# Linear attention and a two-layer FFN on one core: VectorE's first stage in written order, the key sums of nine pairs on TensorE, the second stage's first x chunk fetched and cast in the first stage

## The chip, the cores and the metric

One core of a Trainium2 chip runs the whole kernel. The metric is device time in microseconds of one execution, the median of several runs. Five engines share the core's on-chip memory: TensorE (PE, with its weight loads PEld), VectorE (DVE), ScalarE (ACT), GpSimd (POOL) and SyncE (SP), which here only issues DMAs. Each engine works its own instructions off in the order in which the program put them there, and waits for others by semaphores.

## The reference

```python
def phi(x):
    proj = einsum('bhsd,df->bhsf', x, w_phi)
    proj = proj - max(abs(proj), axis=-1)
    return concatenate([exp(proj), exp(-proj)], axis=-1)

q_p, k_p = phi(q), phi(k)
kv  = einsum('bhsf,bhsd->bhfd', k_p, v)
z   = sum(k_p, axis=2)
num = einsum('bhsf,bhfd->bhsd', q_p, kv)
den = einsum('bhsf,bhf->bhs', q_p, z)[..., None] + 1e-6
x   = (num / den), heads joined: 4608 tokens x 512
h   = x @ w_in                      # 512 -> 2048
g   = maximum(h, 0) + alpha * minimum(h, 0)
out = g @ w_out                     # 2048 -> 512
```

There are 8 batches of 8 heads, 576 tokens a head, head width 64, 128 features (256 with both signs). All data is float32.

## The kernel before, in words

The kernel has two stages, and works on transposed data (features on the 128 partitions, tokens along the free side).

**Attention.** Two heads of a batch make a pair: 32 pairs, four to a batch. `attention_units` (L192) returns a pair's work as small units, each with a due time in units of one pair (the table `AT`, L57). For pair i these stand at i plus:

- `load` (-0.95): keys and queries (`raw`, 576 KB) and values (`v`) from memory.
- `project` (five chunks, at 0 to 0.60, L202): TensorE multiplies token tiles by `w_phi` into one of two PSUM buffers `pj`; VectorE takes the largest magnitude of each row (`m`, L221) and subtracts it (`t`, L222), which frees the buffer. Chunks 0, 1 and 2 hold the k tiles (4 + 1 with 64 rows), chunks 2, 3 and 4 the queries.
- `k_exp` (0.30 and 0.48): ScalarE writes exp(t) and exp(-t) to `xk` (one buffer, L236) and to `k4` (the fifth k tile, two buffers, its lower half zero).
- `k_sum` (0.50, L241): VectorE adds the five k tiles to one, in three additions, `y` (128x1024), `z` and `z` (128x512).
- `k_acc` (0.90, L250): TensorE accumulates kv over the five tiles. `k_z` (1.150, L263): a matmul with a matrix of ones for each head turns `z` into the sums over tokens, in the same PSUM tile.
- `kv_out` (1.153), `kv_turn` (1.52), `q_exp` (1.66 to 1.80): copies and transposes; `qf` (two buffers) holds the features of the queries.
- `den` (2.149) and `num` (2.152): the denominators and numerators of the pair. ScalarE copies the denominators, and SyncE sends them through a transfer to a 128x9 layout (`d9`, L326) in the same unit.
- `invert` (2.50, L329): VectorE adds EPS and takes the reciprocal; SyncE writes it to memory (`rec_d`, L334) and reads it back broadcast over the partitions (`rr`, two transfers, L337).
- `finish` (2.85, L341): GpSimd multiplies (VectorE for the last pair), SyncE stores the pair's part of x (`x_d`, L344).

**FFN, first part.** Numbers enter matmuls as two rounded parts (`rnd` and `low`, L92 and L97), so that each product takes three matmuls (L372 to L374 up, L378 to L380 down). Of the 16 blocks of d_ff the first five (`NF1`) are taken by `ffn1_units` (L382), for chunks of 512 tokens: `fetch` loads x of the chunk (`xr`, one buffer, 1 MB, L388), `split` casts it in four parts (`xh` on VectorE, L395, `xl` on GpSimd, L397), 20 steps `up` and 20 steps `down` follow, three matmuls each; after the last `up` of a block `act_g` (L158) issues two Relus on ScalarE, a combination on VectorE (L163), a cast on ScalarE and a subtraction on VectorE. The results go to `part_d`. Chunks 0 to 6 run in the first stage, spread between the attention units: chunk c starts at `max(4c + FB, F0 + c*FR)` (9.0, 12.3, 15.6, 18.9, 22.8, 26.8, 30.8), its fetch `FL` = 0.5 and its split `FX` = 0.25 ahead.

**Weights.** They come as 64-bit numbers, in half blocks of 256 columns: `decode_load` (L122, `raww`, two buffers), and `decode` (L129): a scaling on ScalarE, four integer instructions on VectorE (L139 to L142), an addition on GpSimd, a cast on ScalarE, a subtraction on GpSimd, and for later blocks a store to `w_d`. In the first stage 20 half blocks are due every 0.5 from 0.55 on, and 20 more between 11 and 31, each load 0.5 ahead.

**The order.** All units go to one list, `todo` (L437), sorted by due time and issued in that order (L455). `tc.manual_schedule` (L456) keeps TensorE and SyncE in just this order. On the other engines the compiler's own scheduler orders the instructions, except where `keep_in_program_order` names one.

**Second stage.** `load_x(0)` (L484, L510) loads the first chunk of x in four transfers and casts it: `rnd` on ScalarE, `low` on VectorE. `pass2` (L547) then runs `up2` and `down2` over the other 11 blocks for nine chunks; after the first block of chunk 0, chunks 7 and 8 of the first part and more weight decoding follow (L560). `load_w2` (L461) brings stored weights back through GpSimd's queue.

Of the kernel before, what the change touches and what calls it, by code (L numbers as in the profile page):

```python
# [55 lines left out]
QH_BUFS = 2  # L56
AT = dict(  # L57
# [3 lines left out]
    ks=0.50,  # L61
# [7 lines left out]
    dv=2.50,  # L69
    x=2.85,  # L70
)
F0 = 9.0
FR = 3.3
FB = 6.8
FL = 0.5
FX = 0.25
# [3 lines left out]
def fused_kernel(ctx: ExitStack, tc: tile.TileContext, kq, v, w_phi, w_in, w_out, alpha, out):  # L80
# [48 lines left out]
    def decode(ff, z, o, n):  # L129
        tag = f"w{ff}_{z}_{o}"  # L130
        if (ff, z, o) not in wraw:
            decode_load(ff, z, o, n)
        raw = wraw.pop((ff, z, o))
        cs = slice(o, o + n)
        lo, hi = raw[:, :, 0], raw[:, :, 1]
        a = w1t.tile([P, n], U32, tag="wa", name=f"a{tag}", bufs=W_BUFS)
        e = w1t.tile([P, n], U32, tag="we", name=f"e{tag}", bufs=W_BUFS)
        act.activation(f(a), hi.bitcast(F32), AF.Copy, scale=2.0**-112)
        dve.tensor_scalar(a, a, 3, None, op0=ALU.logical_shift_left)  # L139
        dve.scalar_tensor_tensor(a, hi, 0x80000000, a, op0=ALU.bitwise_and, op1=ALU.bitwise_or)  # L140
        dve.tensor_scalar(e, a, 0xFF800000, None, op0=ALU.bitwise_and)
        dve.scalar_tensor_tensor(f(e), lo, 2.0**-52, f(e), op0=ALU.mult, op1=ALU.mult)  # L142
        pool.tensor_tensor(f(a), f(e), f(a), op=ALU.add)
        if ff in W:
            th, tl = W[ff][2 * z][:, cs], W[ff][2 * z + 1][:, cs]
        else:
            t = w1t.tile([P, 2, n], F32R, tag="wo", name=f"o{tag}", bufs=1)
            th, tl = t[:, 0, :], t[:, 1, :]
        rnd(act, th, f(a))
        low(pool, tl, f(a), th)  # L150
        if ff not in W:
            nc.sync.dma_start(w_d[ff - NF1, :, 2 * z : 2 * z + 2, cs], f(t))
# [5 lines left out]
    def act_g(ps, ff, n, gp, bufs, tag, el, g_bufs=G_BUFS):  # L158
        r = gp.tile([P, n], F32, tag="r", name=f"r{tag}", bufs=G_BUFS)
        g = gp.tile([P, n], F32, tag="g", name=f"g{tag}", bufs=g_bufs)  # L160
        act.activation(r, ps, AF.Relu, scale=-1.0)  # L161
        act.activation(g, ps, AF.Relu)  # L162
        dve.scalar_tensor_tensor(g, r, aln[:, ff : ff + 1], g, op0=ALU.mult, op1=ALU.add)  # L163
        gh = gp.tile([P, n], F32R, tag="gh", name=f"gh{tag}", bufs=bufs)
        gl = gp.tile([P, n], F32R, tag="gl", name=f"gl{tag}", bufs=bufs)
        rnd(act, gh, g)
        low(el, gl, g, gh)
        return gh, gl
# [23 lines left out]
    def attention_units(i):  # L192
# [48 lines left out]
        def k_sum():  # L241
            x = c["x", 0].rearrange("p a h n f -> p (a h) (n f)")
            y = wk.tile([P, 4, 2 * FD], F32, tag="y", name=f"y{i}", bufs=1)
            z = wk.tile([P, 4, FD], F32, tag="z", name=f"z{i}", bufs=1)
            dve.tensor_tensor(y, x[:, :, : 2 * FD], x[:, :, 2 * FD :], op=ALU.add)
            dve.tensor_tensor(z, y[:, :, :FD], y[:, :, FD:], op=ALU.add)
            dve.tensor_tensor(z, z, c["x", 1].rearrange("p a h n f -> p (a h) (n f)"), op=ALU.add)
            c["z"] = z.rearrange("p (a h) f -> p a h f", a=2)
# [62 lines left out]
        def den():  # L311
            ps_d = ps_m.tile([P, HS], F32, tag="m", name=f"d{i}")
            for a in range(2):
                for g in range(4):
                    h, u = divmod(g, 2)
                    pe.matmul(
                        ps_d[32 * g : 32 * g + 32, :],
                        lhsT=c["st"][:, 2 + a, h * D : h * D + 32],
                        rhs=c["qf"][:, h, a, u * HS : (u + 1) * HS],
                        start=a == 0,  # L320
                        stop=a == 1,
                    )
            d = st.tile([P, HS], F32, tag="d", name=f"ds{i}", bufs=1)
            act.copy(d, ps_d)
            d9 = st.tile([P, 9], F32, tag="d9", name=f"d9_{i}")
            nc.sync.dma_start(d9, d.rearrange("(g r) (p j) -> g r p j", r=32, j=9)[:, 0])  # L326
            c["d9"] = d9

        def invert():  # L329
            d9 = c["d9"]  # L330
            r9 = st.tile([P, 9], F32, tag="r9", name=f"r9_{i}")
            tc.keep_in_program_order(dve.tensor_scalar(d9, d9, EPS, None, op0=ALU.add))
            dve.reciprocal(r9, d9)
            nc.sync.dma_start(rec_d[i].rearrange("(p j) -> p j", j=9), r9)  # L334
            c["r"] = st.tile([P, S], F32, tag="r", name=f"rr{i}", bufs=2)
            for h in range(2):
                nc.sync.dma_start(  # L337
                    c["r"][h * D : (h + 1) * D], rec_d[i : i + 1, h * S : (h + 1) * S].broadcast_to([D, S])
                )

        def finish():  # L341
            e = dve if i == NPAIR - 1 else pool
            e.tensor_tensor(c["s"], c["s"], c["r"], op=ALU.mult)  # L343
            nc.sync.dma_start(x_d[hp, :, b * S : (b + 1) * S], c["s"])  # L344
# [9 lines left out]
            (AT["ks"], k_sum),  # L354
            (AT["kr"], kv_turn),
            (AT["n"], num),
            (AT["d"], den),
            (AT["dv"], invert),
            (AT["x"], finish),
        ]  # L360
# [21 lines left out]
    def ffn1_units(c):  # L382
# [7 lines left out]
        def split():  # L390
            xh = xhl.tile([P, NK, C2], F32R, tag="xh", name=f"xh1_{c}", bufs=1)
            xl = xhl.tile([P, NK, C2], F32R, tag="xl", name=f"xl1_{c}", bufs=1)
            for n in range(NK - 1, -1, -1):
                ins = rnd(dve, xh[:, n], xr[0][:, n])
                if c < B - 2:  # L395
                    tc.keep_in_program_order(ins)
                last[0] = low(pool, xl[:, n], xr[0][:, n], xh[:, n])  # L397
            gs.append([(xh[:, j], xl[:, j]) for j in range(NK)])

        cur = {}  # L400

        def up(ff, n):
            if n == 0:
                cur["ps"] = psf.tile([P, C2], F32, tag="f", name=f"h1_{c}_{ff}")
            ps = cur["ps"]
            gemm1(ps, W[ff], gs[0], (n,))
            if n == NK - 1:
                gs.append(act_g(ps, ff, C2, g1p, GB, f"1_{c}_{ff}", dve, 3))

        def down(m, ff):  # L410
# [6 lines left out]
            o = g1p.tile([P, C2], F32, tag="g", name=f"os1_{c}_{m}", bufs=3)  # L417
            act.copy(o, ps)
            nc.sync.dma_start(part_d[m, :, cs], o)

        steps = [lambda ff=ff, n=n: up(ff, n) for ff in range(NF1) for n in range(NK)]
        steps += [lambda m=m, ff=ff: down(m, ff) for m in range(NK) for ff in range(NF1)]
        return [fetch, split], steps

# [11 lines left out]

    todo = []  # L437
    for i in range(NPAIR):
        todo += attention_units(i)
    for b in range(B - 1):  # L440
        fl, fu = ffn1_units(b)
        t0, t1 = (max(c * NP + FB, F0 + c * FR) for c in (b, b + 1))
        todo += [(t0 + (t1 - t0) * n / len(fu), u) for n, u in enumerate(fu)]
        todo += [(t0 - FL, fl[0]), (t0 - FX, fl[1])]
    first = [(ff, z, o) for z in range(2) for ff in range(NF1) for o in range(0, 512, WN)]
    for n, blk in enumerate(first):
        t = WA + WS * n
# [33 lines left out]
    xs, prt, po = {}, {}, {}  # L481
    x2b = []

    def load_x(c):  # L484
        cs = slice(c * C2, (c + 1) * C2)
        xs[c] = []
        if c > 0:
            xr4 = x2b[0].tile([P, NK, C2], F32, tag="xr", name=f"xr{c}")
            ld_ = nc.sync.dma_start(xr4, x_d[:, :, cs].rearrange("k p s -> p k s"))
            if c > 1:  # L490
                tc.keep_in_program_order(ld_)
        for j in range(NK):
            if c > 0:
                xr = xr4[:, j]
            else:
                xr = x2p.tile([P, C2], F32, tag="xr", name=f"xr{c}{j}", bufs=NK)
                nc.sync.dma_start(xr, x_d[j, :, cs])
# [12 lines left out]
    load_x(0)  # L510
# [7 lines left out]
    def up2(c, ff):  # L518
        ps = psf.tile([P, C2], F32, tag="f", name=f"h2_{c}_{ff}")
        gemm1(ps, W[NF1 + ff], xs[c])  # L520
        gq[c, ff] = act_g(ps, NF1 + ff, C2, x2p, G2_BUFS, f"2_{c}_{ff}", dve)
# [38 lines left out]
    for c in range(B - 1, NC2):  # L560
        loads, units = ffn1_units(c)
        if c == B - 1:
            for u in loads:
                u()
# [3 lines left out]
        else:  # L568
            tail += loads + units
# [58 lines left out]
```

## Time and profile before

| what | us |
|---|---|
| median of 3 runs | 1289.01 (1287.61 to 1291.89) |
| the profiled execution | 1286.31 |
| its span, first to last instruction | 1284.5 |
| PE busy | 1201.5 |
| VectorE busy | 661.7 |
| ScalarE busy | 553.7 |
| GpSimd busy | 205.1 |

Groups, waits and stretches all come from the one profiled execution. A group's line names the line of code, the engine and the operation, then the tile written and the tiles read, shapes, count, total and mean. A line of the waits names who waited for what: total us, times, longest. In a timeline stands the start, the duration, the engine and the instruction, and in brackets the idle time of the engine before it and what ended that. A stretch gives its length, then for PE, PEld, DVE, ACT and POOL the busy time with the count of instructions, then the granted TensorE clock as a share of full speed, the DMA share and GB/s.

Matmuls overlap in the records: one is shown as about 0.4 us, and starts follow each other closer than that.

### The profile page before, as it was taken

Reading aid. Unit: us, or ns where it says so; the run is one execution under the profiler, and the core shown is the slowest. Engines: PE = TensorE matmul, PEld = TensorE weight load, DVE = VectorE, ACT = ScalarE, POOL = GpSimd, SP = SyncE. Lnnn points to the kernel's source line nnn. Section 1 sums busy time; section 2 is a strip of 40 time slices with the busy share of each in tenths; the row PEclk is TensorE's granted clock in tenths of the full one; section 3 lists DMA queues with packets and bytes.
Section 4 is the critical chain, followed back from the end, with each engine's and each line's share of the span. In section 5 each row is a group of like instructions: output and inputs, shape, how many; then the busy total and the mean of one; then the engine's idle time right before and its main releaser. Section 6 shows DMA issues by size and latency. Waiting matters only on the chain.

```text
span 1284.5 us, 16532 instructions
## 1 busy us (share of the span) xinstructions
PE 1201.5 (94%) x6272; PEld 909.1 (71%) x6272; DVE 661.7 (52%) x1134; ACT 553.7 (43%) x1113; POOL 205.1 (16%) x209
## 2 busy tenths in 40 slices
PE   6888699989999899998959999999999999999998
PEld 4555467667766577665647888888888888888886
DVE  6678766656665665667715275333333242324232
ACT  4556455535555454454623364333333233333332
POOL 2223412121130301315404043000000000000000
PEclk9999899999999899999979999999999999999999
DMA  4244425243433524435254141211202020202010
GB/s 160 82 128 140 131 91 159 91 158 100 159 99 117 175 77 147 128 111 180 80 199 148 41 140 58 75 57 42 98 1 99 1 99 1 98 1 99 1 66 33
DMA packets 67806, 124.18 MB, mean 97 GB/s; under 512 B 14224, under 2 KB 19472, under 8 KB 67088
## 3 DMA queue, kind: packets, MB, share of 16 engines
q1 hardware_dynamic: 67008, 117.90, 28.3%
q0 software_dynamic: 720, 5.24, 1.1%
q8 instruction: 49, 0.80, 0.3%
q14 instruction: 29, 0.24, 0.1%
HBM read 89.27 MB, written 33.70 MB: 96 GB/s over the span
## 4 chain that ended last, share of the span: by engine, by line
PE 67%; DVE 13%; DMA 12%; ACT 3%; issue 3%; POOL 2%; SPq 1%; DVEq 0%; ACTq 0%; POOLq 0%
PE h L372 9%; PE h L374 9%; PE h L373 9%; PE po L378 7%; PE po L379 7%; PE po L380 7%; PE pj L213 5%; PE kv L255 3%; DMA xr<-x_d 3%; DMA rr<-rec_d 2%; DVE t L222 2%; DMA raww<-w_out_dram 2%; DVE m L221 2%; DMA raww<-w_in_dram 2%; DMA rec_d<-r 2%
## 5 line engine op out<-in xcount | busy, mean ns | idle before, releaser
L163 DVE SCALAR_TENSOR_TENSOR g<-r,aln,g 128x512 f32<-128x512 f32 x144 | 112.4, 781 | 289.3 <-ACT g L162 287.5
L161 ACT ACTIVATE r<-h 128x512 f32<-128x512 f32 x144 | 86.0, 597 | 271.4 <-PE h L374 271.3
L213 PE MATMUL pj<-w_sb,raw 128*128 128x256 f32 x576 | 158.8, 400 | 43.8 <-DVE t L222 37.1
L213 PEld LDWEIGHTS pj<-w_sb,raw 128*128 128x128 f32 x576 | 109.1, 196 | 74.8 <-issue 46.2
L378 PE MATMUL po<-gh,w 128*128 128x512 f32 x396 | 155.2, 392 | 0.0
L379 PE MATMUL po<-gh,w 128*128 128x512 f32 x396 | 155.1, 392 | 0.0
L380 PE MATMUL po<-gl,w 128*128 128x512 f32 x396 | 153.2, 392 | 0.0
L98 DVE TENSOR_TENSOR gl<-g,gh 128x512 fp32r<-128x512 f32 x144 | 105.4, 732 | 74.1 <-ACT gh L94 73.5
L94 ACT CAST gh<-g 128x512 fp32r<-128x512 f32 x144 | 89.6, 622 | 101.5 <-DVE g L163 101.1
L221 DVE TENSOR_REDUCE m<-pj 128x4 f32<-128x512 f32 (+1 forms) x160 | 100.3, 628 | 23.1 <-PE pj L213 22.4
L222 DVE TENSOR_TENSOR t<-pj,m 128x512 f32<-128x512 f32 (+1 forms) x160 | 100.8, 631 | 2.1
L372 PE MATMUL h<-xh,w 128*128 128x512 f32 x180 | 88.1, 489 | 13.2 <-DVE xh L95 13.2
L372 PE MATMUL h<-x2hl,w 128*128 128x512 f32 x220 | 87.0, 396 | 13.9 <-ACT x2hl L94 13.9
L343 POOL TENSOR_TENSOR s<-s,rr 128x576 f32<-128x576 f32 x31 | 44.5, 1434 | 281.7 <-DMA rr<-rec_d 272.1
L378 PE MATMUL o<-gh,w 128*128 128x512 f32 x180 | 85.4, 475 | 2.6 <-ACT gh L94 1.6
L373 PE MATMUL h<-x2hl,w 128*128 128x512 f32 x220 | 86.6, 394 | 0.0
L374 PE MATMUL h<-x2hl,w 128*128 128x512 f32 x220 | 86.6, 394 | 0.0
L380 PEld LDWEIGHTS po<-gl,w 128*128 128x128 f32 x396 | 74.3, 188 | 16.7
L379 PEld LDWEIGHTS po<-gh,w 128*128 128x128 f32 x396 | 74.3, 188 | 16.7
L378 PEld LDWEIGHTS po<-gh,w 128*128 128x128 f32 x396 | 74.3, 188 | 16.7
L162 ACT ACTIVATE g<-h 128x512 f32<-128x512 f32 x144 | 85.6, 595 | 0.0
L294 ACT ACTIVATE qf<-qt 128x512 f32<-128x512 f32 x128 | 68.8, 599 | 30.5 <-PE qt L292 30.3
(77 smaller groups left out, 2084.6 us busy)
## 6 DMA issues: line engine op xcount, KB each, us to landing
raw<-kq_dram SPq DMA_DIRECT2D x32, 576.0 KB
xr<-x_d SPq DMA_DIRECT2D x17, 1024.0 KB
v<-v_dram SPq DMA_DIRECT2D x32, 320.0 KB
rr<-rec_d SPq DMA_DIRECT2D x64, 144.0 KB
x_d<-s SPq DMA_DIRECT2D x32, 288.0 KB
part_d<-os SPq DMA_DIRECT2D x36, 256.0 KB
pt<-part_d SPq DMA_DIRECT2D x9, 1024.0 KB
raww<-w_in_dram SPq DMA_DIRECT2D x32, 256.0 KB
```

The source lines that it names most:

```text
L94: return act.copy(dst, src)
L98: return eng.tensor_tensor(dst, src, f(hi), op=ALU.subtract)
L163: dve.scalar_tensor_tensor(g, r, aln[:, ff : ff + 1], g, op0=ALU.mult, op1=ALU.add)
L213: pe.matmul(ps[:, j].rearrange("p h f -> p (h f)"), lhsT=c["raw"][:, tp * P : (tp + 1) * P], rhs=w_sb, start=True, stop=True,)
L221: dve.tensor_reduce(m, ps, axis=AX.X, op=ALU.max, apply_absolute_value=True)
L222: dve.tensor_tensor(c["t", ch][:, :, j0 : j0 + w].rearrange("p h j f -> p j h f"), ps, m.unsqueeze(3).broadcast_to([P, w, 2, FD]), op=ALU. ...
L372: pe.matmul(ps, lhsT=wt[0][:, ws], rhs=xh, start=n == 0, stop=False)
L373: pe.matmul(ps, lhsT=wt[1][:, ws], rhs=xh, start=False, stop=False)
L374: pe.matmul(ps, lhsT=wt[0][:, ws], rhs=xl, start=False, stop=n == NK - 1)
L378: pe.matmul(ps, lhsT=wt[2][:, ws], rhs=gh, start=first, stop=False)
L379: pe.matmul(ps, lhsT=wt[3][:, ws], rhs=gh, start=False, stop=False)
L380: pe.matmul(ps, lhsT=wt[2][:, ws], rhs=gl, start=False, stop=last)
```

## The change

Six edits, all in the first stage but for the last call:

1. `tc.manual_schedule` now names VectorE too: it runs the sorted list in written order. For this, units are cut: `k_sum` into three steps (0.50, 0.64, 0.84), `split` into four (0.44, 0.36, 0.28 and 0.20 ahead of the chunk), `act_g` into `parts` (with the matmuls), `join` (0.10 later) and `rest` (0.20 later), `decode` into `decode_scale` (0.14 ahead), `decode_split` and `decode_store` (0.40 later).
2. For pairs below `ZP` = 9 `k_sum` does nothing, and `k_z` multiplies each of the five k tiles by ones: ten matmuls a pair for two.
3. DMAs become units of their own: `den_out` (2.44), `invert` with the `rec_d` store (2.68), `spread` (`rr`, 2.88), `finish` (3.12), `store` (3.26), and the store of `part_d` 0.14 after its step.
4. The chunks start later: `F0` 9.2 and `FB` 7.1 give 9.2, 12.5, 15.8, 19.1, 23.1, 27.1 and 31.1, with the fetch 0.60 ahead.
5. `finish` of the last pair is on GpSimd as for the others.
6. The second stage's first x chunk is fetched at 31.2, in one transfer into the buffer `xr` of the FFN chunks, and cast in four units at 32.35, 32.45, 33.3 and 33.4 into the two `qf` buffers; `load_x(0)` and its four transfers are gone.

```diff
+ZP = 9
-    ks=0.50,
+    ks=(0.50, 0.64, 0.84),
...
-    dv=2.50,
-    x=2.85,
+    d9=2.44,
+    dv=2.68,
+    rr=2.88,
+    x=3.12,
+    xs=3.26,
 )
-F0 = 9.0
+F0 = 9.2
 FR = 3.3
-FB = 6.8
-FL = 0.5
-FX = 0.25
+FB = 7.1
+FL = 0.60
+FX = (0.44, 0.36, 0.28, 0.20)
+FG = (0.10, 0.20)
+FS = 0.14
+WE = 0.14
+X0T = (31.2, 32.35, 32.45, 33.3, 33.4)
+WO = 0.40
...
+        def k_sum(step):
+            if i < ZP:
+                return
...
         def k_z():
-            for h in range(2):
-                pe.matmul(
-                    c["kv"][h * D : (h + 1) * D, 1], lhsT=ones, rhs=c["z"][:, :, h, :], start=False, stop=True
-                )
+            if i < ZP:
+                zs = [c["x", 0][:, :, :, j, :] for j in range(4)] + [c["x", 1][:, :, :, 0, :]]
+            else:
+                zs = [c["z"]]
+            for j, z in enumerate(zs):
+                for h in range(2):
+                    pe.matmul(
+                        c["kv"][h * D : (h + 1) * D, 1],
+                        lhsT=ones,
+                        rhs=z[:, :, h, :],
+                        start=False,
+                        stop=j == len(zs) - 1,
+                    )
...
         def finish():
-            e = dve if i == NPAIR - 1 else pool
-            e.tensor_tensor(c["s"], c["s"], c["r"], op=ALU.mult)
+            pool.tensor_tensor(c["s"], c["s"], c["r"], op=ALU.mult)
+
+        def store():
             nc.sync.dma_start(x_d[hp, :, b * S : (b + 1) * S], c["s"])
...
+    def first_x():
+        st = {}
+
+        def fetch0():
+            st["xr"] = xhl.tile([P, NK, C2], F32, tag="xr", name="xr2_0", bufs=XR_BUFS)
+            nc.sync.dma_start(st["xr"], x_d[:, :, :C2].rearrange("k p s -> p k s"))
+            xs[0] = []
+
+        def cast0(j):
+            if j % 2 == 0:
+                st["xq"] = qp.tile([P, 2, 2, S], F32R, tag="qf", name=f"x2hl0{j}", bufs=QH_BUFS)
+            xh, xl = (st["xq"][:, n, j % 2, :C2] for n in range(2))
+            rnd(act, xh, st["xr"][:, j])
+            low(dve, xl, st["xr"][:, j], xh)
+            xs[0].append((xh, xl))
+
+        return [fetch0] + [lambda j=j: cast0(j) for j in range(NK)]
...
+        for n, us in enumerate(fu):
+            todo += [(t0 + (t1 - t0) * n / len(fu) + dt, u) for dt, u in us]
+        todo.append((t0 - FL, fetch))
+        todo += [(t0 - dt, u) for dt, u in zip(FX, splits)]
...
+        todo.append((t - WE, lambda blk=blk: decode_scale(*blk, WN)))
+        todo.append((t, lambda blk=blk: decode_split(*blk, WN)))
+        todo.append((t + WO, lambda blk=blk: decode_store(*blk, WN)))
+    todo += [(t, u) for t, u in zip(X0T, first_x())]
     todo.sort(key=lambda tu: tu[0])
-    with tc.manual_schedule(engines={mybir.EngineType.PE, mybir.EngineType.SP}):
+    with tc.manual_schedule(engines={mybir.EngineType.PE, mybir.EngineType.SP, mybir.EngineType.DVE}):
...
-    load_x(0)
     with tc.issue_after(last[0].ins):
         load_w2(range(N2A))
```

More of the change, by code (lines that the diff above doesn't have):

```diff
@@ L127, in decode_load, with decode_scale @@
         wraw[ff, z, o] = raw
[L129 removed]
+    wst = {}
+    def decode_scale(ff, z, o, n):
         tag = f"w{ff}_{z}_{o}"
@@ L133, in decode, with decode_split @@
         raw = wraw.pop((ff, z, o))
+        a = w1t.tile([P, n], U32, tag="wa", name=f"a{tag}", bufs=W_BUFS)
+        act.activation(f(a), raw[:, :, 1].bitcast(F32), AF.Copy, scale=2.0**-112)
+        wst[ff, z, o] = raw, a
+    def decode_split(ff, z, o, n):
+        tag = f"w{ff}_{z}_{o}"
+        raw, a = wst.pop((ff, z, o))
+        lo, hi = raw[:, :, 0], raw[:, :, 1]
         cs = slice(o, o + n)
-        lo, hi = raw[:, :, 0], raw[:, :, 1]
-        a = w1t.tile([P, n], U32, tag="wa", name=f"a{tag}", bufs=W_BUFS)
         e = w1t.tile([P, n], U32, tag="we", name=f"e{tag}", bufs=W_BUFS)
-        act.activation(f(a), hi.bitcast(F32), AF.Copy, scale=2.0**-112)
         dve.tensor_scalar(a, a, 3, None, op0=ALU.logical_shift_left)
@@ L148, in decode, with decode_store @@
             th, tl = t[:, 0, :], t[:, 1, :]
+            wst[ff, z, o] = t
         rnd(act, th, f(a))
         low(pool, tl, f(a), th)
-        if ff not in W:
-            nc.sync.dma_start(w_d[ff - NF1, :, 2 * z : 2 * z + 2, cs], f(t))
+    def decode_store(ff, z, o, n):
+        if (ff, z, o) in wst:
+            t = wst.pop((ff, z, o))
+            nc.sync.dma_start(w_d[ff - NF1, :, 2 * z : 2 * z + 2, o : o + n], f(t))
+    def decode(ff, z, o, n):
+        decode_scale(ff, z, o, n)
+        decode_split(ff, z, o, n)
+        decode_store(ff, z, o, n)
     W = {ff: weight_tile(w1p, f"w{ff}")[0] for ff in range(NF1)}
@@ L158, in act_g, with parts, join, rest @@
     def act_g(ps, ff, n, gp, bufs, tag, el, g_bufs=G_BUFS):
[L159 to L168, printed above, removed]
+        st = {}
+        def parts():
+            st["r"] = gp.tile([P, n], F32, tag="r", name=f"r{tag}", bufs=G_BUFS)
+            st["g"] = gp.tile([P, n], F32, tag="g", name=f"g{tag}", bufs=g_bufs)
+            act.activation(st["r"], ps, AF.Relu, scale=-1.0)
+            act.activation(st["g"], ps, AF.Relu)
+        def join():
+            g = st["g"]
+            dve.scalar_tensor_tensor(g, st["r"], aln[:, ff : ff + 1], g, op0=ALU.mult, op1=ALU.add)
+            st["gh"] = gp.tile([P, n], F32R, tag="gh", name=f"gh{tag}", bufs=bufs)
+            rnd(act, st["gh"], g)
+        def rest():
+            gl = gp.tile([P, n], F32R, tag="gl", name=f"gl{tag}", bufs=bufs)
+            low(el, gl, st["g"], st["gh"])
+            return st["gh"], gl
+        return parts, join, rest
     qp = ctx.enter_context(tc.tile_pool(name="qp", bufs=2))
@@ L353, in attention_units @@
             (AT["q"][1], lambda: q_exp(1)),
-            (AT["ks"], k_sum),
+            *((AT["ks"][n], lambda n=n: k_sum(n)) for n in range(3)),
             (AT["kr"], kv_turn),
@@ L357, in attention_units @@
             (AT["d"], den),
+            (AT["d9"], den_out),
             (AT["dv"], invert),
+            (AT["rr"], spread),
             (AT["x"], finish),
+            (AT["xs"], store),
         ]
@@ L388, in fetch, with split @@
             nc.sync.dma_start(xr[0], x_d[:, :, cs].rearrange("k p s -> p k s"))
[L390 to L400, printed above, removed]
+        xt = []
+        def split(n):
+            if not xt:
+                xt.append(xhl.tile([P, NK, C2], F32R, tag="xh", name=f"xh1_{c}", bufs=1))
+                xt.append(xhl.tile([P, NK, C2], F32R, tag="xl", name=f"xl1_{c}", bufs=1))
+            xh, xl = xt
+            j = NK - 1 - n
+            rnd(dve, xh[:, j], xr[0][:, j])
+            last[0] = low(pool, xl[:, j], xr[0][:, j], xh[:, j])
+            if n == NK - 1:
+                gs.append([(xh[:, j], xl[:, j]) for j in range(NK)])
+        cur, ga = {}, {}
         def up(ff, n):
@@ L416, in down, with out1 @@
                 return
[L417 to L423, printed above, removed]
+            cur["o", m] = g1p.tile([P, C2], F32, tag="g", name=f"os1_{c}_{m}", bufs=3)
+            act.copy(cur["o", m], ps)
+        def out1(m):
+            nc.sync.dma_start(part_d[m, :, cs], cur["o", m])
+        steps = []
+        for ff in range(NF1):
+            for n in range(NK):
+                steps.append([(0, lambda ff=ff, n=n: up(ff, n))])
+            steps[-1].append((FG[0], lambda ff=ff: ga[ff][1]()))
+            steps[-1].append((FG[1], lambda ff=ff: gs.append(ga[ff][2]())))
+        for m in range(NK):
+            for ff in range(NF1):
+                steps.append([(0, lambda m=m, ff=ff: down(m, ff))])
+            steps[-1].append((FS, lambda m=m: out1(m)))
+        return fetch, [lambda n=n: split(n) for n in range(NK)], steps
     def merge(a, b_):
@@ L486, in load_x @@
         xs[c] = []
[L487 to L491, printed above, removed]
-        for j in range(NK):
[L493 to L497, printed above, removed]
+        xr4 = x2b[0].tile([P, NK, C2], F32, tag="xr", name=f"xr{c}")
+        ld_ = nc.sync.dma_start(xr4, x_d[:, :, cs].rearrange("k p s -> p k s"))
+        if c > 1:
+            tc.keep_in_program_order(ld_)
+        for j in range(NK):
+            xr = xr4[:, j]
             if j % 2 == 0:
@@ L520, in up2 @@
         gemm1(ps, W[NF1 + ff], xs[c])
-        gq[c, ff] = act_g(ps, NF1 + ff, C2, x2p, G2_BUFS, f"2_{c}_{ff}", dve)
+        parts, join, rest = act_g(ps, NF1 + ff, C2, x2p, G2_BUFS, f"2_{c}_{ff}", dve)
+        parts()
+        join()
+        gq[c, ff] = rest()
     def down2(c, ff):
@@ L560, in fused_kernel @@
     for c in range(B - 1, NC2):
-        loads, units = ffn1_units(c)
+        fetch, splits, steps = ffn1_units(c)
+        units = [u for us in steps for _, u in us]
         if c == B - 1:
-            for u in loads:
+            for u in [fetch] + splits:
                 u()
@@ L568, in fused_kernel @@
         else:
-            tail += loads + units
+            tail += [fetch] + splits + units
     merge(tail, decode_units(range(NA, NA + ND)))
```

52 lines of the change are left out of this document (27 added, 25 removed).

## The prediction

> **What bounds the kernel now.** I read the page first, then a table by stretches, then TensorE's waits, then the timeline at the places that the waits named.
>
> ```profile
> PE 1201.5 (94%) x6272; PEld 909.1 (71%) x6272; DVE 661.7 (52%) x1134; ACT 553.7 (43%) x1113; POOL 205.1 (16%) x209
> ```
>
> TensorE (PE) is the engine to fill: 1201.5 of 1284.5 us, and no other engine is above 52%. The stretches are chosen at the first pair's end, the first FFN chunk, the last attention pair and the border between the stages:
>
> ```profile
> 36.00:134.00 98.00, 82.28 (x568) 55.23 (x568) 73.36 (x148) 56.10 (x125) 28.58 (x30) 0.95 0.40 126
> 134.00:153.00 19.00, 10.33 (x57) 5.54 (x53) 11.65 (x19) 3.77 (x11) 9.79 (x9) 0.73 0.51 163
> 153.00:646.00 493.00, 466.82 (x2848) 331.06 (x2847) 319.88 (x562) 257.20 (x546) 117.87 (x111) 0.98 0.40 124
> 646.00:658.00 12.00, 11.35 (x50) 8.93 (x48) 0.39 (x2) 2.73 (x5) 1.43 (x1) 1.00 0.45 139
> 658.00:675.00 17.00, 3.79 (x10) 2.98 (x11) 4.67 (x8) 2.39 (x5) 0.72 (x1) 0.60 0.61 204
> ```
>
> Read the first two numbers (length, PE busy) and the one after POOL's, the granted clock. PE idles 15.7 us in the first stretch, 8.7 in the second, 26.2 in the long one, 13.2 at the border; beyond 675 us it is full, and the change does nothing there. The clock is below 1 just where PE idles, so each wait costs twice. What PE waited for, over the whole run, and until 153 us:
>
> ```profile
> PE pj L213 <- DVE t L222: 37.1, 23, 5.1
> PE h L372 <- ACT x2hl L94: 13.9, 1, 13.9
> PE h L372 <- DVE xh L95: 13.2, 4, 8.4
> ```
>
> ```profile
> PE pj L213 <- DVE t L222: 18.4, 12, 3.2
> PE h L372 <- DVE xh L95: 8.4, 1, 8.4
> ```
>
> So the projection's two PSUM buffers wait for VectorE's subtraction (18.4 us among the first pairs, 37.1 - 18.4 = 18.7 later); chunk starts wait for the cast of x (8.4 at the first, 4.8 later); the second stage waits once, 13.9. VectorE is not full, so this is its order. At 67 us:
>
> ```profile
> 67.26 0.43 DVE L221 TENSOR_REDUCE m<-pj 128x2 f32<-128x256 f32 x1
> 68.75 1.22 DVE L245 TENSOR_TENSOR y<-xk 128x1024 f32<-128x1024 f32 x1 [1.06 <-ACT xk L238]
> 69.89 0.42 DVE L222 TENSOR_TENSOR t<-pj,m 128x256 f32<-128x256 f32 x1
> ```
>
> ```profile
> 70.46 0.76 PE L213 MATMUL pj<-w_sb,raw 128*128 128x256 f32 x1 [2.09 <-DVE t L222]
> ```
>
> The key sum y stands between the maximum m and the subtraction t of one chunk; it first waits 1.06 us for ScalarE, then runs 1.22, and PE waits 2.09 for t.
>
> **Part 1: z of nine pairs on TensorE.** VectorE loses three instructions a pair, grouped here over the first 153 us (nine pairs):
>
> ```profile
> L245 DVE TENSOR_TENSOR y<-xk 128x1024 f32<-128x1024 f32 x9 | 13.0, 1445 | 3.2 <-ACT xk L238 3.2
> ...
> L246 DVE TENSOR_TENSOR z<-y 128x512 f32<-128x512 f32 x9 | 6.3, 697 | 0.0
> L247 DVE TENSOR_TENSOR z<-z,k 128x512 f32<-128x512 f32 x9 | 6.1, 683 | 0.1
> ```
>
> That is 25.4 us of VectorE. TensorE's two z matmuls a pair become ten; each is two instructions, so 16 more a pair, shaped like those that accumulate kv:
>
> ```profile
> 104.33 2.03 PE L255 MATMUL kv<-xk,v 128*64 128x256 f32 x16
> 106.20 0.60 PE L255 MATMUL kv<-k,v 128*64 128x256 f32 x4
> ```
>
> Sixteen of them hold the array from 104.33 to 106.20, 1.87 us; nine pairs: **+16.8 us** of PE on the path. Bounds: 9 x 2.03 = 18.3 if nothing overlaps, and 15 if a fifth falls into waits that stay. Against it, the 18.4 us of waits on t: with y gone and the order written m, t, m, t, I take 14 as removed (bounds 8 and 18.4; what stays is VectorE itself being late). Another lock appears: xk has one buffer, and k_z now reads it, so ScalarE's next exponentials wait until k_z of the pair before, at 1.15, where k_acc at 0.90 freed it. Behind them on ScalarE stand the copies of n and ks; PE needs the result only at k_acc, three projection chunks and the transposes later, and the exponentials were issued after that point in this trace too. I cost it at nothing; without that cover it is one xk pair, about 2 us, for each of eight pairs.
>
> **The clock.** Two neighbouring stretches of one pair each:
>
> ```profile
> 66.00:83.00 17.00, 14.08 (x90) 9.72 (x91) 12.22 (x27) 10.30 (x21) 4.78 (x5) 0.90 0.32 104
> 83.00:96.00 13.00, 11.57 (x88) 7.57 (x87) 10.14 (x20) 6.47 (x17) 3.82 (x5) 1.00 0.46 147
> ```
>
> The pair with the 2.09 us wait got a clock of 0.90, the next 1.00. From 36 to 153 us the clock lost 0.05 x 98 + 0.27 x 19 = 10 us, some 2.5 of it inside idle time; of the 7.5 I give back 6 (bounds 2 and 7.5).
> The Trainium skill ("TensorE: Matmul & The Clock Gate", Part 1, What's actually happening) has the clock fall to half only after an idle window of about 3.4 us. By that rule the 2 us waits cost no clock, and only about 2 us would come back instead of 6; the trace disagrees, since the longest wait on t before 153 us is 3.2.
>
> **Part 2: the transfers' order.** In the first FFN chunk PE waited 8.4 us. SyncE's queue ahead of it:
>
> ```profile
> 128.05 0.59 SPq L326 DMA_DIRECT2D d<-ds  x1
> 133.83 0.32 SPq L334 DMA_DIRECT2D rec_d<-r  x1
> 135.29 1.10 SPq L337 DMA_DIRECT2D rr<-rec_d  x2
> 136.45 0.58 SPq L388 DMA_DIRECT2D xr<-x_d  x1
> ```
>
> The x fetch stood behind rec_d, which waited 5 us for VectorE's reciprocal. In the new order the fetch (9.2 - 0.60 = 8.60) comes before rec_d of pair 6 (8.68) and after its d9 (8.44), so it is issued about 6 us sooner, and the chunk starts 0.2 of a pair later, behind d, n and z work. Of 8.4 us I take 7 as removed (bounds 3 and 8.4). Sum until 153 us: 16.8 - 14 - 6 - 7 = **-10 us** (bounds +4 and -17).
>
> **Part 3: 153 to 646 us.** The largest wait, 5.1 us, is this:
>
> ```profile
> 275.71 7.22 DMA xr<-x_d
> 282.96 3.56 DVE xh L95 x4
> 287.00 2.05 PE pj L213 x4
> ```
>
> VectorE stood at the four casts while xr was under way, and the projection waited behind. The new order keeps this: a cast 0.16 of a pair (3 us, at 493 us for some 24.5 pairs) behind its fetch still waits 3 to 4 us. Queued behind it are m and t, and PE waits for these. But with the chunks at 23.1, 27.1 and 31.1 the casts stand at 0.66 to 0.90 of a pair, past the last projection (0.60), and there they delay nobody. SyncE's other edits (d9, rec_d, rr, x_d and the weight store as separate units) each move a transfer behind the time when its data is there; their loads reach PE only through the same waits. Join and rest of the activations stand 0.10 and 0.20 behind their matmuls, about the time that ScalarE takes, so VectorE shouldn't stand at them. Of the 26.2 us I take 14, and 4 us of clock (0.02 x 493 = 10 lost): **-18 us** (bounds -6 and -30).
>
> **Part 4: the border.**
>
> ```profile
> 641.43 1.10 SPq L337 DMA_DIRECT2D rr<-rec_d  x2
> 652.89 0.33 SPq L344 DMA_DIRECT2D x_d<-s  x1
> 653.31 0.58 SPq L326 DMA_DIRECT2D d<-ds  x1
> ...
> 663.94 1.77 SPq L497 DMA_DIRECT2D xr<-x_d  x4
> 665.75 14.89 SPq L388 DMA_DIRECT2D xr<-x_d  x2
> ```
>
> The second stage's first x (663.94) needs only pairs long done, but stood behind the last pair's store. Fetched and cast in the first stage, its instructions are these:
>
> ```profile
> L94 ACT CAST x2hl<-xr x20: 614/622/635, 667.4 to 1174.2; 128x512 fp32r<-128x512 f32 x20
> L98 DVE TENSOR_TENSOR x2hl<-xr,x2hl x20: 681/685/693, 668.1 to 1175.3; 128x512 fp32r<-128x512 f32 x20
> ```
>
> Four each, 2.5 and 2.7 us, beside PE's chunk-6 matmuls (without that cover, +2.7). The fetch waits for chunk 6's last GpSimd subtraction to free its buffer; behind it on SyncE stand the rr and x_d transfers of the last four pairs, which only chunk 7 needs. What is late next is chunk 7's x, which needs the last pair: d9 of pair 31 still stands behind the store of pair 30 (33.26 before 33.44), as at 652.89 and 653.31. The last multiplication also goes to GpSimd:
>
> ```profile
> L343 POOL TENSOR_TENSOR s<-s,rr x31: 1395/1419/1737, 47.8 to 651.4; 128x576 f32<-128x576 f32 x31
> ```
>
> So that chain keeps its length (1.4 us more at most) while PE gets to fill it 24 matmuls of the second stage (12 up, 12 down; 11.35 us for 50 in the stretch before 658 us, so 0.227 each: 5.4 us) and three of chunk 6's steps moved behind the last pair (2 us). With 1.8 us of half clock saved, **-9 us** (bounds -4, where the chain grows, and -14, all of the idle time).
>
> **Sum.** -10 - 18 - 9 = -37. The profiled execution took 1286.3 us (span 1284.5, and 1.8 around it): 1249. The median of the runs is 2.7 above it: **1252 us**.
>
> **Rivals.** *Waits only move (1277 us).* The z matmuls take what the first pairs gain, and the casts standing at their fetch keep most of the later waits: 0 - 6 - 6 = -12. For it speaks the row at 282.96, against it that y's place alone explains the 2 us waits. *Nearly all waits close (1230 us):* -17 - 30 - 12 = -59; VectorE's share of half the span speaks for it, its fixed order against. *Slower (1314 us): VectorE stands at the weight blocks.* In written order it must wait at a block's split for ScalarE, which waits for the block:
>
> ```profile
> ACT aw L138 <- DMA raww<-w_in_dram: 56.4, 22, 7.3
> ```
>
> That is 2.6 us a block (56.4 / 22), and this stage has 40 blocks, 104 us. If the second projection buffer covers two fifths of it (my estimate), PE loses 62, less the 37: +25. It decides from 0.9 us of PE a block (37 / 40). Against it: the split stands half a pair behind its load, 7 to 10 us, and the wait is ScalarE's, not yet VectorE's.
>
> **How the numbers follow.** Forecast 0.56, moved waits 0.22, closed waits 0.15, slower 0.07. The forecast's own range is 1238 to 1268; with most of the two faster rivals it is 1236 to 1280, leaving out the slower one and the outer part of the closed one. A difference under 0.3% (3.9 us) can't be told from none: faster 0.88, same 0.05, slower 0.07.
>
> **What would show it.** Right: no y before 150 us, waits of pj on t until 153 us under 5 us, PEclk at 0.97 or more there, the chunk-0 wait under 2 us, the border wait under 8 us and no longer on x2hl. Wrong: VectorE idle on aw with pj waiting behind it, n's pairs still 15 us apart in the first nine, or the wait on xh at the border as long as that on x2hl was.

## The result and the profile after

The changed kernel takes 1252.63 us (median of 4, 1247.12 to 1254.26) against 1288.31 (median of 4): a ratio of 0.9711, 95% interval 0.9675 to 0.9748. 1252 was forecast. The total came out as predicted. Of its three parts the first came near its forecast, the middle gained nearly twice its forecast, and the border lost where a gain was forecast: that the total is right is luck. The profiled execution took 1254.26 us, its span 1252.0.

From the page of the changed kernel:

```profile
PE 1210.5 (97%) x6416; PEld 914.7 (73%) x6416; DVE 655.3 (52%) x1106; ACT 551.6 (44%) x1113; POOL 204.5 (16%) x210
PE   7899999999999999999969999999999999999998
...
PEclk9899999999999999999988999999999999999999
```

TensorE has its 144 more instructions, 9 us more busy time, and one dent left, at the border. VectorE's busy time fell by 6.4 us, not by 25, since others of its instructions take longer now (not followed further). What TensorE waited for:

```profile
PE qt_t L337 <- ACT sf L329: 8.2, 6, 2.5
PE h L431 <- DVE xh L104: 7.9, 1, 7.9
PE pj L248 <- DMA raw<-kq_dram: 6.1, 1, 6.1
PE o L437 <- ACT g L190: 3.1, 1, 3.1
PE pj L248 <- DVE t L257: 2.9, 5, 0.7
```

The waits of the projection on t went from 37.1 us to 2.9, and the waits on xh are one, at the border. A new one stands first: the transpose qt_t waits for ScalarE's copy sf. To see where the time went I cut both traces at the same pieces of work: where the numerators of pair 0, of pair 7 and of pair 31 end. Pair 7's end at 152.8 us in the kernel before, which is the 153 us of the prediction. I call the three stretches the first part, the middle and the end. Before:

```profile
35.10:152.80 117.70, 93.31 (x625) 61.22 (x623) 85.67 (x168) 60.19 (x134) 38.36 (x39) 0.91 0.41 131
152.80:646.20 493.40, 467.22 (x2851) 331.29 (x2849) 320.08 (x562) 257.40 (x546) 117.87 (x111) 0.98 0.40 125
646.20:1284.50 638.30, 616.02 (x2666) 500.42 (x2664) 231.63 (x357) 221.71 (x406) 40.74 (x42) 0.99 0.19 66
```

After:

```profile
36.40:148.80 112.40, 102.16 (x731) 65.80 (x729) 69.52 (x144) 55.99 (x130) 34.47 (x38) 0.94 0.42 135
148.80:608.70 459.90, 457.45 (x2846) 326.30 (x2846) 320.00 (x536) 254.66 (x534) 106.31 (x96) 1.00 0.41 131
608.70:1252.00 643.30, 621.78 (x2674) 503.88 (x2673) 245.21 (x386) 225.39 (x420) 56.08 (x59) 0.99 0.20 68
```

The first part became 5.3 us shorter, the middle 33.5 shorter, and the end 5.0 longer. Nearly all of the gain lies in the middle: there TensorE's idle time (length less busy time) fell from 26.2 to 2.5 us, and the clock, at 0.98 before, is full. Since the chunks start later, about 1.5 us of chunk work moves behind the first cut and 2 us behind the last; this is an estimate, from the prediction's 0.227 us a matmul.

A single execution must not be read too closely in the first part. The experiment nb2 has the same first stage, since its edit begins only behind the last pair, and its stretches are these:

```profile
34.40:139.10 104.70, 97.37 (x731) 63.95 (x729) 70.47 (x143) 56.14 (x130) 32.90 (x37) 0.98 0.42 135
139.10:600.00 460.90, 457.42 (x2848) 326.41 (x2846) 318.14 (x537) 254.80 (x534) 107.58 (x98) 1.00 0.41 133
600.00:1243.00 643.00, 623.24 (x2675) 504.93 (x2673) 241.89 (x386) 225.48 (x420) 55.02 (x59) 0.99 0.20 68
```

The first part varies by 8 us between these two executions, the middle and the end by 1 us or less.

### The profile page after: what moved, and what is told of

It reads as the page before. It is cut to its first block, busy times and chain, and to the rows that moved or that the text cites. A ratio compares the mean times of both kernels' runs of the same rounds, so it can differ in the third digit from the quotient of the medians.

```text
span 1252.0 us, 16787 instructions
## 1 busy us (share of the span) xinstructions
PE 1210.5 (97%) x6416; PEld 914.7 (73%) x6416; DVE 655.3 (52%) x1106; ACT 551.6 (44%) x1113; POOL 204.5 (16%) x210
## 4 chain that ended last, share of the span: by engine, by line
PE 83%; DMA 6%; DVE 4%; ACT 3%; issue 2%; POOL 1%; SPq 1%; DVEq 0%; POOLq 0%; ACTq 0%
PE h L431 10%; PE h L433 10%; PE h L432 10%; PE pj L248 7%; PE po L437 7%; PE po L438 7%; PE po L439 7%; PE kv L297 5%; PE n L353 4%; PE o L437 3%; PE o L438 3%; PE o L439 3%; DMA raww<-w_out_dram 2%; PE d L367 2%; DMA rr<-rec_d 2%; PE kv L312 2%
## 5 line engine op out<-in xcount | busy, mean ns | idle before, releaser
L248 PE MATMUL pj<-w_sb,raw 128*128 128x256 f32 x576 | 154.4, 392 | 9.1 <-DMA raw<-kq_dram 6.1
L439 PE MATMUL o<-gl,w 128*128 128x512 f32 x180 | 71.4, 399 | 1.0 <-DVE gl L107 1.0
```

The costliest lines, as they stand in the source:

```text
L248: pe.matmul(ps[:, j].rearrange("p h f -> p (h f)"), lhsT=c["raw"][:, tp * P : (tp + 1) * P], rhs=w_sb, start=True, stop=True,)
L439: pe.matmul(ps, lhsT=wt[2][:, ws], rhs=gl, start=False, stop=last)
```

## Experiments

Ratios are to the kernel before, run on the same chip; a hundredth is 12.9 us. The last three columns are the lengths of the three stretches in us, each from the one profiled execution of that kernel.

| kernel | ratio | 95% interval | first part | middle | end |
|---|---|---|---|---|---|
| the kernel before | 1 | | 117.7 | 493.4 | 638.3 |
| the changed kernel | 0.9711 | 0.9675 to 0.9748 | 112.4 | 459.9 | 643.3 |
| z0: no z on TensorE | 0.9703 | 0.9676 to 0.9729 | 100.4 | 465.2 | 642.9 |
| auto_dve: VectorE not in written order | 0.9705 | 0.9680 to 0.9730 | 103.1 | 468.9 | 637.9 |
| late_x: no early x | 0.9722 | 0.9693 to 0.9751 | 107.7 | 469.5 | 638.6 |
| z0_auto: neither z nor written order | 0.9754 | 0.9726 to 0.9782 | 107.7 | 470.4 | 640.9 |
| old_chunks: chunk times of before | 0.9780 | 0.9752 to 0.9808 | 107.3 | 471.8 | 636.4 |
| old_dma: transfers' units and times of before | 0.9913 | 0.9886 to 0.9941 | 99.0 | 492.1 | 643.2 |
| dma_only: these transfers, little else | 0.9899 | 0.9871 to 0.9928 | 104.2 | 496.2 | 636.2 |
| before_z9: before, with z of nine pairs | 1.0102 | 1.0076 to 1.0128 | 125.7 | 495.5 | 636.8 |
| z32: z of all pairs on TensorE | 0.9971 | 0.9953 to 0.9988 | 109.4 | 497.9 | 636.2 |
| nb2: two blocks in the border | 0.9696 | 0.9670 to 0.9721 | 104.7 | 460.9 | 643.0 |
| tail_order: written order behind the first stage too | 0.9807 | 0.9779 to 0.9834 | 105.4 | 460.4 | 656.6 |
| auto_tail_nb2: a candidate | 0.9877 | 0.9847 to 0.9906 | 104.9 | 467.6 | 657.0 |

### The parts that the change names, taken away singly

After the trace, my theory (A) was that VectorE's written order had closed the waits, and that z on TensorE hardly paid. Its rival (B) was the prediction's own account.

z0:

```diff
-ZP = 9
+ZP = 0
```

> The changed kernel with ZP = 0: VectorE adds the k tiles for all 32 pairs, in written order. Theory A (the written order closes the waits, the z matmuls hardly pay): -8 to +2 us against the changed kernel's 1252.6, since TensorE gets 16.8 us back in the first nine pairs and y no longer stands between m and t. Rival B (it is VectorE's relief of 25 us that closes the first pairs' waits): +5 to +15 us, with waits of pj on t back above 8 us before 153 us.

Measured: 0.9703 against 0.9711, no difference. Both accounts were half right. Until 145 us the projection's waits on t are back:

```profile
PE pj L248 <- DVE t L257: 17.0, 14, 3.1
```

but TensorE has, by the prediction's price, 16.8 us less to do: what the z matmuls buy is about what they cost.

z32:

```diff
-ZP = 9
+ZP = 32
```

> The changed kernel with ZP = 32: z of all pairs from all k tiles on TensorE. If TensorE is the bound from the first chunk on (theory A), each of the 23 further pairs costs its 1.87 us: +38 to +43 us, about 1293. Rival (VectorE's relief of 2.6 us a pair gives part back): +10 to +30 us.

Measured: 0.9971, 0.026 or 33 us above the changed kernel, 1.5 us for each of the 23 further pairs. That lies between the two accounts. The middle alone, where these pairs are, takes 497.9 us against 459.9, or 1.6 us a pair, which is the first account's price; the end is 7 us shorter (see The border). So TensorE is the bound there, and VectorE's relief gives little back. The projection's waits on t stay at 3.2 us in all, so little was there to be had.

auto_dve:

```diff
-mybir.EngineType.SP, mybir.EngineType.DVE}):
+mybir.EngineType.SP}):
```

> The changed kernel with VectorE left to the compiler's scheduler, all else kept. Theory A (the written order is the main gain): +20 to +35 us, with waits of pj on t back at 15 us or more after 153 us. Rival (the separate transfer units and the later chunk times made the gain): 0 to +8 us.

Measured: 0.9705, no difference. Theory A, as an account of the total, fell. The compiler's order leaves 17.4 us of waits on t, where the written one leaves 2.9, and yet the kernel is as fast: in that trace there is no wait on sf among the longest ones, and the border waits 3.3 us for xh, not 7.9. Equal totals do not mean that the written order does nothing: the middle takes 459.9 to 465.2 us in four traces with it and the new transfer and chunk times (the changed kernel, nb2, tail_order and z0; late_x, told of next, apart), and 467.6 to 470.4 in three without it (auto_dve, z0_auto and auto_tail_nb2). What it gains there, auto_dve gets back in the first part and at the end.

late_x:

```diff
+    load_x(0)
     with tc.issue_after(last[0].ins):
         load_w2(range(N2A))
...
-    todo += [(t, u) for t, u in zip(X0T, first_x())]
```

(with `load_x` as before). 

> The changed kernel without the early fetch and casts: the second stage's first x chunk is loaded and cast behind the first stage, as before. The prediction's term says +9 us (+4 to +14). The trace after says that chunk 7's x ends the border either way (7.9 us wait on xh) and that new waits follow: by that +2 to +6 us.

Measured: 0.9722, no difference. The wait on the second stage's x is back:

```profile
PE h L431 <- ACT x2hl L103: 11.5, 1, 11.5
```

The other border waits are gone in exchange: behind the last pair this trace takes 1252.1 - 613.5 = 638.6 us, the changed kernel's 643.3. But the test is not clean. With this edit 50 of the 64 half blocks of weights are scaled before the last pair's end, in the changed kernel 42, and the middle is 9.6 us longer, with 5.1 us of waits on t behind 500 us where the changed kernel has 0.7.

So no part that stands in the change's title changes the total measurably when taken away alone. The gain had to lie in the parts that come with them: the transfers as units of their own, and the later chunk times.

### The parts that come with them

z0_auto is z0 and auto_dve together.

> The changed kernel with neither: ZP = 0 and VectorE left to the compiler's scheduler; the transfer units, chunk times and the early x stay. Taken away singly, neither cost anything that could be measured (1249.1 and 1249.8 us). Theory C (transfer units and chunk times are the gain, both edits on VectorE are idle): 1245 to 1254. Rival D (written order and z stand in for each other, either closes the first pairs' waits): 1258 to 1268, waits of pj on t above 15 us before 150 us.

Measured: 0.9754. It lies between the two expectations, at 1255.65 us: about 5 us above z0 and auto_dve, whose intervals (up to 0.9729 and 0.9730) just touch this one's (from 0.9726). The waits on t until 145 us are 22.0 us here, 17.0 in z0 and 6.8 in auto_dve. By the totals, written order and z stand in for each other, with about 5 us at stake, at the edge of the noise; 31 of the 36 us are left without either. The first part fits rival D, being 7.3 us longer here than in z0 and 4.6 longer than in auto_dve, though it varies by 8 us between executions; the middle adds 5.2 and 1.5.

old_dma:

```diff
-    d9=2.44,
-    dv=2.68,
-    rr=2.88,
-    x=3.12,
-    xs=3.26,
+    d9=2.1495,
+    dv=2.50,
+    rr=2.50,
+    x=2.85,
+    xs=2.85,
...
-FS = 0.14
+FS = 0.0
-WO = 0.40
+WO = 0.0
```

> The changed kernel with every transfer issued again in the unit and at the time of before (d9 with den, rec_d and rr at 2.50, finish and store at 2.85, weight and part_d stores at once), VectorE in written order. Theory C1 (the separate transfer units are the gain): +15 to +30 us against 1252.6, with PE waiting on xh at chunk starts. Rival C2 (the later chunk times with the earlier fetch are): 0 to +6 us.

Measured: 0.9913, 0.020 or 26 us above the changed kernel: the largest part, as C1 says. In the profile all of the loss is in the middle, 492.1 us against 459.9, and the first part is even shorter. The edit moves six kinds of transfers at once (d9, rec_d, rr, x_d, part_d and w_d); what each is worth was not told apart. The queue of SyncE shows how the fetch of x is held. In this trace, ahead of chunk 6 (SyncE, then VectorE, then TensorE):

```profile
578.29 0.33 SPq L387 DMA_DIRECT2D rec_d<-r  x1
579.74 1.11 SPq L392 DMA_DIRECT2D rr<-rec_d  x2
580.95 0.53 SPq L484 DMA_DIRECT2D part_d<-os  x1
581.52 0.43 SPq L447 DMA_DIRECT2D xr<-x_d  x1
```

```profile
589.96 2.17 DVE L104 CAST xh<-xr 128x512 fp32r<-128x512 f32 x3 [8.70 <-DMA xr<-x_d]
```

```profile
590.44 0.80 PE L431 MATMUL h<-xh,w 128*128 128x512 f32 x1 [4.95 <-DVE xh L104]
```

The fetch is due 0.60 of a pair ahead of its chunk here too, but rec_d of pair 28 falls due at that time, 30.50, and waits for VectorE's reciprocal; rr waits for rec_d's landing. The fetch comes behind both, VectorE, now bound to its order, stands 8.70 us at the cast, and TensorE waits 4.95. In the changed kernel, at the same chunk:

```profile
563.25 0.46 SPq L447 DMA_DIRECT2D xr<-x_d  x1
...
570.13 0.42 DVE L104 CAST xh<-xr 128x512 fp32r<-128x512 f32 x1
```

The fetch goes out before rec_d, the cast starts 6.9 us later without a wait, and the first matmul at 575.20, 12 us behind the fetch (8.9 in old_dma, 6.8 in the kernel before). VectorE's waits on xr between 140 and 610 us, in old_dma and in the changed kernel:

```profile
DVE xh L104 <- DMA xr<-x_d: 40.9, 6, 8.7
```

```profile
DVE xh L104 <- DMA xr<-x_d: 1.5, 2, 0.8
```

old_chunks:

```diff
-F0 = 9.2
+F0 = 9.0
-FB = 7.1
+FB = 6.8
-FL = 0.60
-FX = (0.44, 0.36, 0.28, 0.20)
+FL = 0.5
+FX = (0.25, 0.25, 0.25, 0.25)
```

> The changed kernel with F0, FB, FL and FX of before (chunks 0.2 to 0.3 of a pair sooner, fetch 0.5 ahead, all four casts 0.25 ahead). Theory C2: +10 to +25 us, waits on xh at chunk starts and of pj on t behind the casts back at 10 us or more. Theory C1: 0 to +6 us.

Measured: 0.9780, 0.007 or 9 us above. The waits on t are 10.6 us in all, and those on xl 2.5, and the middle is 11.9 us longer: the casts, closer behind their fetch and all at one place, hold the projection again. The profiled execution is the fastest of its six (1252.37 us, the median is 1259.89), so it shows the loss only in part. This is the second part of the gain, smaller than C2 had it.

dma_only keeps just the transfers' units and times: ZP = 0, VectorE left to the compiler, chunk times and x load as before, and

```diff
-    ks=(0.50, 0.64, 0.84),
+    ks=(0.50, 0.50, 0.50),
...
-FG = (0.10, 0.20)
+FG = (0.0, 0.0)
-WE = 0.14
+WE = 0.0
```

> Nearly one part alone on top of the kernel before: the transfers as units of their own at the new times. VectorE is left to the compiler, z is on VectorE for all pairs, the chunk times and the x load of the second stage are those of before, and the cut steps stand at one time again. Theory C1 (these units are the main gain): 1260 to 1270, 20 us or more below before, with the waits on xh at chunk starts under 6 us. Rival (they only work together with the later chunks): 1276 to 1288.

Measured: 0.9899, 13 us below before; neither account, it lies between. The fetch now leads its chunk by 11 to 22 us and no wait on xh is left at the chunk starts, but the compiler puts the four casts in a row ahead of the projection's m and t. VectorE, then TensorE, at chunk 2:

```profile
256.22 0.69 DVE L257 TENSOR_TENSOR t<-pj,m 128x512 f32<-128x512 f32 x1
260.60 3.61 DVE L104 CAST xh<-xr 128x512 fp32r<-128x512 f32 x4 [3.69 <-DMA xr<-x_d]
264.13 2.30 DVE L282 TENSOR_TENSOR y<-xk 128x1024 f32<-128x1024 f32 x1
```

```profile
269.74 0.77 PE L248 MATMUL pj<-w_sb,raw 128*128 128x256 f32 x1 [4.55 <-DVE t L257]
```

So the transfers alone give 13 us, in the profile all of it in the first part: the middle takes 496.2 us here, 493.4 in the kernel before. Adding the chunk times, the spread casts and other cut steps, and the early x (z0_auto) gives 19 more, of which the early x is nothing that late_x could find. In the middle, then, the transfers pay only together with the later chunks and spread casts: without the one (old_dma) all of its gain is lost, and without the other (dma_only) there is none.

before_z9 is the kernel before with the diff of `k_sum` and `k_z` alone.

> The kernel before with z of the first nine pairs on TensorE and nothing else. The prediction's terms, 16.8 us more on TensorE against 14 us of waits and 6 of clock: 1288.5 - 3, that is 1282 to 1290. If y's place is not what holds the projection there: 1298 to 1305. If VectorE's relief runs through to the first chunk: 1272 to 1280.

Measured: 1.0102, slower by 13 us: 1299.88, the number of the second account, but not for its reason. Without the rest of the change, z on TensorE is a loss, although it does close the first pairs' waits on t. TensorE's waits in this kernel's first 160 us:

```profile
PE qt_t L298 <- ACT sf L290: 9.5, 6, 2.8
PE h L384 <- DVE xh L96: 8.9, 1, 8.9
PE pj L214 <- DMA raw<-kq_dram: 5.5, 1, 5.5
PE kt L288 <- ACT ks L283: 5.3, 5, 1.5
PE pj L214 <- DVE t L223: 2.0, 3, 1.2
```

Of the 18.4 us on t 2.0 are left, and 14.8 us of waits for copies of ScalarE, which the kernel before didn't have there, stand in their place. So the z matmuls' 16.8 us come on top. In the changed kernel's trace such a wait is easily followed (ScalarE, then TensorE):

```profile
86.62 0.45 ACT L146 ACTIVATE aw<-raww 128x256 f32<-128x256 f32 x1 [0.98 <-DMA raww<-w_out_dram]
86.97 0.39 ACT L360 COPY s<-n 128x288 f32<-128x288 f32 x1
88.73 0.43 ACT L146 ACTIVATE aw<-raww 128x256 f32<-128x256 f32 x1 [1.37 <-DMA raww<-w_out_dram]
89.07 0.71 ACT L268 ACTIVATE k<-t 64x256 f32<-64x256 f32 x2
89.69 0.56 ACT L329 COPY sf<-kt 128x512 f32<-128x512 f32 x1
```

```profile
90.30 0.65 PE L337 MATMUL qt_t<-ident,t 128*128 128x128 f32 x2 [2.22 <-ACT sf L329]
```

The copy sf, which frees the buffer for qt_t, stands behind two weight scalings, and these wait for the loads of their weight blocks (0.98 and 1.37 us). In the changed kernel's first 153 us all four waits on sf above 0.3 us look like this. It is the slower rival's wait, on ScalarE instead of VectorE. It takes more than z on TensorE: z0, without it, has no waits on copies of ScalarE there, but old_dma, with it and the old transfers, has only 2.1 us of them. That earlier weight loads would remove the waits was not tried.

### The border

Theory E was that the weight blocks, which the compiler now puts ahead of chunk 7's casts and activations, eat the border's gain. In the changed kernel's trace ScalarE stands there:

```profile
627.01 0.71 ACT L103 CAST w<-aw 128x256 fp32r<-128x256 f32 x2 [7.93 <-DMA x_d<-s]
...
629.39 0.58 ACT L189 ACTIVATE r<-h 128x512 f32<-128x512 f32 x1
```

A weight cast waits for the last x_d store, and behind it the Relu of the second stage's first block, whose matmuls had ended at about 624.6. In the kernel before, 50 of the 64 half blocks are scaled by the end of the last pair; in the changed kernel 42 are, and six more follow in the next 50 us.

tail_order:

```diff
-    merge(tail, decode_units(range(NA, NA + ND)))
+    with tc.manual_schedule(engines={mybir.EngineType.Activation, mybir.EngineType.DVE}):
+        merge(tail, decode_units(range(NA, NA + ND)))
```

> The changed kernel with VectorE and ScalarE kept in written order also behind the first stage, where the weight blocks are merged with the chunks 7 and 8. Theory E (the compiler's early weight blocks stand in front of chunk 7's casts and activations and eat the border's gain): -5 to -9 us, 1244 to 1248. Rival (the border is set by chunk 7's x alone): -2 to +3 us.

Measured: 0.9807, slower by 0.010. Theory E isn't supported, though the test was not clean: the new order brought waits of its own,

```profile
PE h L431 <- DVE xh L104: 8.6, 2, 8.3
PE h L431 <- ACT g L190: 8.1, 5, 2.5
```

apparently since the cast of one activation, in written order, now stands ahead of the next one's Relus on ScalarE. The wait on xh is as long as in the changed kernel, although fewer weight blocks stand ahead of it.

nb2:

```diff
-NB = 1
+NB = 2
```

> The changed kernel with two blocks of the second stage, not one, between the first stage and chunk 7 (NB = 2): 24 more matmuls, 5.4 us, stand in the wait for chunk 7's x. Rival to theory E (chunk 7's x alone sets the border): -4 to -8 us. Theory E: 0 to -3 us, the waits move to the activations behind.

Measured: 0.9696 against 0.9711: not to be told apart, although the median, 1245.11, is the lowest of all. Its span behind the last pair, 1243.0 - 600.0 = 643.0 us, is the changed kernel's. The border keeps a wait of 6.2 us, now on a copy of ScalarE.

auto_tail_nb2 puts auto_dve, tail_order and nb2 together.

> A candidate for a faster version: VectorE left to the compiler in the first stage, written order for VectorE and ScalarE behind it, NB = 2, z of nine pairs on TensorE, all transfer edits kept. If the three gains of the traces add: 1236 to 1243. If they stand in for each other: 1245 to 1252.

Measured: 0.9877, worse than either expectation: the gains don't add, and the loss of the written order behind the first stage stays. What sets the border's last 10 us is left open: that it isn't the early x (late_x's total, z32's end) and isn't mended by either edit is shown, that ScalarE's waiting weight cast is its cause is only argued. The weight blocks do go with it: the five profiled executions with 50 half blocks ahead of the last pair's end (the kernel before, late_x, dma_only, before_z9 and z32, of which z32 has the early x) take 636 to 639 us for the end, the seven with 42 take 636 to 643. That fits theory E and doesn't prove it; tail_order, with 40, is among the slowest.

## Why the prediction was right in sum and wrong in its parts

**Until 153 us, -10 forecast.** Measured: -5.3 in the profile, -13.0 in that of nb2. The z matmuls' price was near: 1.87 us a pair forecast, 1.5 measured over 23 pairs in z32. The waits on t closed as said (18.4 to 1.2 us), and so did chunk 0's wait (8.4 to nothing), the fetch being issued ahead of rec_d. The step that failed is a term that the sum doesn't have: behind the closed waits, TensorE waits 10.2 us for ScalarE's copies sf and s, which stand behind weight scalings. "I cost it at nothing" was said of the lock on xk alone, and of that it holds: in these 153 us TensorE waits for none of ScalarE's exponentials, and none of them is recorded as waiting for the z matmuls. The clock rose from 0.91 to 0.94, about 4 us of the 6 forecast (0.98 and 8 us in nb2). One sign of being wrong came true: the pairs' numerators are still 16.1 us apart (15.0 in nb2, 16.8 before). The bounds, +4 and -17, hold the z matmuls at 16.8 us; with their own bounds they are +5 and -19.

**The middle, -18 forecast.** Measured: -33.5, beyond the bound of -30. Here the step was "their loads reach PE only through the same waits", with which I gave SyncE's edits no price of their own, and "the new order keeps this". With the old transfers the middle is 32 us longer (old_dma). I had read the right row, the fetch behind rec_d, and applied it to chunk 0 alone; in the kernel before all seven fetches stood close behind a small transfer that waits for an engine: rec_d and rr at chunks 0 and 1, the weight store w_d at 2 and 3, part_d at 4 to 6. From issue to first matmul it was 6 to 13 us there. I also had the casts stand at the fetch for 3 to 4 us, due 0.16 of a pair behind it; but VectorE reaches them later than they are due (6.9 us behind the fetch at chunk 6), when x has landed, and its waits on xr between 140 and 610 us fell from 14.2 us to 1.5. TensorE's idle time fell by 23.7 us where 14 were forecast, and the clock, 0.98 to 1.00 over 493 us, gave most of the other 10, where 4 were forecast.

**The border, -9 forecast.** Wrong in its sign: +5 in the profile, of which about 2 are chunk work moved there, and nothing by late_x. That chunk 7's x would be late next was right, and also its chain (d9 of pair 31 stands behind the store of pair 30 in both). The failed step is that 24 matmuls would fill the wait. TensorE ran the twelve up, and the twelve down came behind chunk 7's first four steps, at 637.93, after a wait of 7.9 us; later, a wait of 3.1 us and some of about 1 us stand where the kernel before has one of 1.6.

**The sum.** The middle's 15 us too little and the border's 14 us too much cancelled. The total is right by luck, not by the working.

**Rivals.** Moved waits: true of the border, and of 10.2 of the 25.6 us that closed until 153 us. Closed waits: true of the middle. The slower one showed up on ScalarE, in the waits on sf; VectorE itself stood at a scaling for 5.6 us in the first stage, four times, where that rival had 104.

**The clock.** Around the wait of 2.22 us that ended at 90.30, in the changed kernel:

```profile
86.00:90.30 4.30, 1.83 (x12) 1.23 (x11) 3.80 (x10) 2.31 (x7) 0.88 (x2) 1.00 0.24 69
90.40:93.80 3.40, 3.40 (x16) 1.86 (x18) 0.00 (x0) 2.39 (x7) 0.73 (x1) 0.50 0.03 1
93.80:100.00 6.20, 6.20 (x54) 3.77 (x52) 4.09 (x7) 0.40 (x1) 1.59 (x2) 1.00 0.82 283
```

TensorE was busy for 1.83 of 4.3 us, and then ran 3.4 us at half clock though it was busy all the time. The rule that the prediction cited from the Trainium skill ("TensorE: Matmul & The Clock Gate", Part 1) wants an idle window of about 3.4 us for that; here the longest wait ahead of it was 2.22 us, in a stretch that is mostly idle. So in this trace shorter waits do go with lost clock, as the prediction took it, and new waits of the same length kept part of my 6 us from coming back.

## What to carry to other kernels

When SyncE's queue is in order, look at what stands ahead of the transfer that a stage waits for, at every chunk and not at one: a small store that waits for an engine can hold a large load behind it. Issuing the transfers as units of their own, so that the load goes out first, was worth more here than any order of the arithmetic, though only together with the chunk times that use it. The small stores still wait: SyncE stands 193.3 us for the reciprocals in the changed kernel's first 640 us, and what changed is what stands behind them. Two edits that might close the same wait have to be undone together before either is called idle. A total that comes out right says nothing on its parts, and two equal totals can be sums of unequal ones; cut the traces at the same piece of work, and compare stretch by stretch.

## What the runs showed of the hardware that was not expected

The same first stage, instruction for instruction on TensorE, took 608.7 us in one profiled execution and 600.0 in another (the changed kernel and nb2), all of the difference within the first eight pairs, where short waits and half-clock stretches go together. And sixteen z instructions cost 1.5 us of the kernel's time (z32), where each is recorded as some 0.4 us: records overlap, and the start of the next instruction is the measure.
